# A visit's scores cut in two around the weighted sums, nine chunks as four rounds of eight tiles and one of four

## The chip, the cores and the metric

The kernel runs on one core of a Trainium2 chip. The metric is the device time of one execution in microseconds, the median of the timed runs. Lower is better.

## What is computed

The reference is a masked attention followed by a two-layer feed-forward network with a softplus between the layers:

```python
scores = scale * np.matmul(q, k.transpose(0, 1, 3, 2))        # B 8, H 8, S 576, D 64
rel = pos[:, None] - pos[None, :]
mask_local = (rel >= 0) & (rel < stride)                      # stride 32, heads 0 to 3
mask_strided = (rel >= 0) & (pos[None, :] % stride == pos[:, None] % stride)   # heads 4 to 7
attn = softmax(np.where(masks, scores, -1e9))
x = (attn @ v).transpose(0, 2, 1, 3).reshape(4608, 512)
h = x @ w_in                                                  # 512 x 2048
g = np.maximum(h, 0.0) + np.log1p(np.exp(-np.abs(h)))
out = g @ w_out                                               # 2048 x 512
```

Each query sees few keys, so the kernel computes only blocks of 32 queries by 64 keys on the diagonal. The host has put the queries and keys of the strided heads in an order in which their mask is such a band too.

## The kernel before

**The network.** The 4608 tokens are nine chunks of 512. A chunk takes 16 steps, one for each 128 columns of `w_in`. A step on TensorE (PE) is `hidden` (line 623: 12 matmuls of 128x512 into a tile `ph`) and, two steps later, `output` (line 663: 12 matmuls of 128x512 into the four tiles `py`). Between them ScalarE (ACT) makes abs, exp and ln of `ph` into `u` (lines 635 to 640), and VectorE (DVE) makes `u` = max(`ph`, 0) + `u` (line 644, the last reader of `ph`), then the rounded part `gh` (line 253) and the rest `gl` (line 656), which `output` reads. `ph` has two buffers (`ps_h`).

**The attention.** Heads are handled in pairs. There are 32 pairs, number n. The first eight are done in a first stage whose order is written out by hand. From n = 8 on a pair is a *visit* that the planner puts between a `hidden` and an `output`: one visit every three steps for n = 8 to 11, every four steps after that. A visit `S{n}` of n > 8 does two things on PE: the scores of pair n (`score_steps`, line 343) and the weighted sums of pair n - 1 (`weighted`, line 519, 12 matmuls for each half of the sequence).

**The scores of a pair.** They are nine chunks. A chunk is four products of 64x32 by 64x64 in fp32: two heads (rows 0 to 63 or 64 to 127 of PE's array) times two places (columns). In the trace each product is two matmuls. `SPLIT = [(0, 6), (6, 9)]`: chunks 0 to 5 go into the tile `ps`, chunks 6 to 8 into the upper half of `po`, whose lower half takes the sums' first half. The second sums' half goes to `pv`, a buffer of `ps_h`. The two parts are issued side by side: chunks 0 and 6, 1 and 7, 2 and 8, then 3, 4 and 5 alone. `place_of` swaps the heads' columns for the second part, so that chunks 0 and 6 together use eight different tiles of the array (two row halves times four column quarters), while a chunk alone uses four.

**Behind the scores** DVE adds the mask to each part (`add_mask`, line 409) into `prob`, takes the row maxima (line 414), subtracts them (line 418); ACT takes exp; DVE sums (line 428), inverts and multiplies (line 440), and turns `prob` into `pt` by transposes of 32 rows (line 451), one for each run of chunks with the same column order: 16 a pair, in two groups of eight with a `u`, `gh`, `gl` behind each. The next visit's sums read `pt`. Behind the sums ACT copies each half to `x_h` (line 557) and DVE writes the rest, `x_l` (line 555). The `ph` of the `hidden` behind the visit's `output` waits for DVE.

**The order.** `Plan` takes tasks with an urgency, an engine, a cost and what they come after, places each at the earliest gap on its engine, and issues all by the start that results. The tasks here are `S{n}` (PE), `Y{n}{j}` (the masks, DVE), `x s E z g R M` (the softmax), `P{n}.{j}` (transposes), `H` and `L` (`x_h` and `x_l`).

Of the kernel before, what the change touches and what calls it, by code (L numbers as in the profile page):

```python
# [10 lines left out]
F32 = mybir.dt.float32  # L11
F32R = mybir.dt.float32r
BF16 = mybir.dt.bfloat16
# [6 lines left out]
P = 128  # L20
# [3 lines left out]

TILE = 96
SPLIT = [(0, 6), (6, 9)]


def block_at(chunk, place):

    return (chunk, 2 * place) if chunk < 6 else (3 * place + chunk - 6, 1)
# [48 lines left out]
class Plan:  # L80
# [8 lines left out]
    def add(self, name, urgency, engine, cost, fn, after=(), late=0.0):  # L89
        self.tasks[name] = (urgency, len(self.tasks), engine, cost, fn, after, late)  # L90
# [29 lines left out]
def attention_softplus_ffn(  # L120
# [9 lines left out]
    nc = tc.nc  # L130
    B, NPAIR, _, _, S = qk.shape
# [7 lines left out]
    NCHK = NTILE * 3 // 2  # L139
# [20 lines left out]

    nc.scalar.preload_act_table_set("natural_log_exp_and_others")
    mask_b = const.tile([P, 12 * 64], BF16, name="mask_b")

# [9 lines left out]
    xs = {}  # L175
# [43 lines left out]
    def is_local(n):  # L219
        return order[n][1] < NPAIR // 2  # L220

    def q_of(n):
        return qT_early[n] if n < NPAIR else qT

    def k_of(n):
        return kT_early[n] if n < NPAIR else kT[n % 2]
# [66 lines left out]

    def mask_of(n, part):

        if is_local(n):
            return mask_b[:, : 6 * 64] if part == 0 else mask_b[:, 64 : 4 * 64]
        if part == 0:
            return mask_b[:, 6 * 64 : 9 * 64].unsqueeze(1).broadcast_to([P, 2, 3 * 64])
        return mask_b[:, 9 * 64 :]  # L300

    def place_of(n, part, h):

        return 1 - h if n >= NPAIR and part == 1 else h

    def score_steps(n, part):

        b = order[n][0]
        masked = b < 2
        if b == 0:  # L310
            ps = py[2 * (n % 2) + part]
        elif b == 1 or part == 0:
            taken.append(n)
            ps = ps_s.tile([P, 512], F32, tag="ps", name=f"ps_{n}_{part}")
        else:
            shared[n] = ps_o.tile([P, 512], F32, tag="po", name=f"po_{n}")
            ps = shared[n][:, S // 2 :]
        pss[n, part] = ps
        lo, hi = SPLIT[part]
        rows = [slice(64 * place, 64 * place + 64) for place in range(2)]  # L320

        def add(first):
            for place in range(2):
                nc.tensor.matmul(  # L324
                    ps[rows[place], : 64 * (hi - lo)],
                    lhsT=ident_b[:, rows[place]],
                    rhs=mask_of(n, part),
                    start=first,
                    stop=not first,
                )  # L330


        if masked and n > 0:
            add(True)
        for x in range(lo, hi):
            yield
            for place in range(2):
                a, i = block_at(x, place)
                c = TILE * a + 32 * i
                for h in range(2):  # L340
                    to = 64 * place + 32 * place_of(n, part, h)
                    head = slice(64 * h, 64 * h + 64)
                    nc.tensor.matmul(  # L343
                        ps[to : to + 32, 64 * (x - lo) : 64 * (x - lo) + 64],
                        lhsT=q_of(n)[head, c : c + 32],
                        rhs=k_of(n)[head, c : c + 64],
                        start=not masked or n == 0 and x == lo,
                        stop=not masked or n > 0 and x == hi - 1,
                    )
        if masked and n == 0:  # L350
            add(False)

    def scores(n, parts=range(2)):

        for _ in zip_longest(*[score_steps(n, part) for part in parts]):
            pass

    def parts(n, part=None):
        if n not in sts:
            sts[n] = st_pool.tile([P, 4, NCHK], F32, tag="stat", name=f"st_{n}")  # L360
        lo, hi = (0, NCHK) if part is None else SPLIT[part]
        sv = None
        if (n, part) in pss:
            sv = pss[n, part][:, : 64 * (hi - lo)].rearrange("p (a c) -> p a c", c=64)
        return prob_of(n)[:, lo:hi], sv, [sts[n][:, i, lo:hi] for i in range(4)]
# [36 lines left out]
    def add_mask(n, j):  # L402
        pv, sv, _ = parts(n, j)
        m = mask_of(n, j)
        if len(m.shape) == 3:
            pv, sv = (x.rearrange("p (two a) c -> p two (a c)", two=2) for x in (pv, sv))
        else:
            m = m.rearrange("p (a c) -> p a c", c=64)
        nc.vector.tensor_tensor(pv, sv, m, op=ALU.add)  # L409
        pss.pop((n, j))  # L410
# [31 lines left out]
    def prob_transposes(n, quarters=range(4)):  # L442
        p = prob_of(n)
        for quarter in quarters:
            for place, h in (divmod(quarter, 2),):
                for part, (lo, hi) in enumerate(SPLIT):
                    row = 64 * place + 32 * place_of(n, part, h)
                    src = p[row : row + 32]
                    a, i = block_at(lo, place)
                    for c in range(2):  # L450
                        nc.vector.transpose(  # L451
                            pt[
                                32 * (i + c) : 32 * (i + c) + 32,
                                h,
                                a : a + hi - lo,
                                32 * i : 32 * i + 32,
                            ],
                            src[:, lo:hi, 32 * c : 32 * c + 32],
                        )
# [42 lines left out]
    def weighted(n, half, joint=False):  # L502


        if joint:
            if half == 0:
                po = shared[n + 1]
            else:
                po = ps_h.tile([P, 512], F32, tag="ph", name=f"pv_{n}")
        elif half == 1 and (n == NPAIR - 1 or n >= 2 * NPAIR):  # L510
            taken.append(n)
            po = ps_s.tile([P, 512], F32, tag="ps", name=f"pv_{n}_{half}")
        else:
            po = ps_o.tile([P, 512], F32, tag="po", name=f"pv_{n}_{half}")
        pos[n, half] = po
        for x in range(NTILE // 2):
            a = NTILE // 2 * half + x
            for h in range(2):
                nc.tensor.matmul(  # L519
                    po[64 * h : 64 * h + 64, TILE * x : TILE * x + TILE],  # L520
                    lhsT=vs[n][:, a, h, :],
                    rhs=pt_of(n, a)[:, h, a % 2],
                    start=True,
                    stop=True,
                )
# [284 lines left out]
    for i in range(begin, len(steps) + LAG):  # L810
# [23 lines left out]
        for t in range(nt):  # L834
            name = f"O{k}" if t == nt - 1 else f"O{k}.{t}"
            after = [f"l{k}", before] + ([f"y{k-1}.{t}"] if f == 0 else [])
            add(name, x + 0.01 * t, "PE", 0.7, lambda c=c, f=f, t=t: output(c, f, (t,)), after)
            before = name
            if k == len(steps) - 1 and t == nt - 1:

                for h, (e, engine) in enumerate((("DVE", nc.vector), ("ACT", nc.scalar))):
                    cols = slice(DM // 2 * h, DM // 2 * (h + 1))
                    fn = lambda c=c, t=t, engine=engine, cols=cols: result(c, t, engine, cols)
                    add(f"y{k}.{t}{h}", x + 0.7 * t + 0.7, e, 0.35, fn, [name])
            elif f == NFC - 1:
                e, cost, engine = (("ACT", 0.5, nc.scalar), ("DVE", 0.6, nc.vector))[t % 2]
                fn = lambda c=c, t=t, engine=engine: result(c, t, engine)
                add(f"y{k}.{t}", x + 0.7 * t + 0.7, e, cost, fn, [name])
    def sums_of(n):
        for half in range(2):  # L850
            weighted(n, half, n != last)

    i_of = {n: i for i, n in pair_at.items()}
    for i, n in pair_at.items():
        x = when[i]
        if n > 2 * NPAIR:
            z = x - (when[i] - when[i - 2] if i - 2 in when else 0.0)
            add(f"Q{n}", z, "ACT", 2.5, lambda n=n: lay_out_q(n), [f"q{n}", f"S{n-1}"])
        after = [f"Q{n}", f"k{n}", f"Y{n-1}0", f"Y{n-1}1", f"L{n-2}1"]
        cost = 1.3  # L860
        if joint(i):
            cost = 2.5
            after += [f"P{n-1}", f"v{n-1}", f"u{i-1}"]

        def work(i=i, n=n):
            scores(n)
            if joint(i):
                sums_of(n - 1)

        add(f"S{n}", x, "PE", cost, work, after)  # L870
        y = x + 1.5
        for j in range(2):
            after = [f"S{n}", f"P{n-2}"]
            add(f"Y{n}{j}", y + j, "DVE", 0.47, lambda n=n, j=j: add_mask(n, j), after)
        after = [f"Y{n}0", f"Y{n}1"]
        for j, (letter, e, cost, fn) in enumerate(
            (
                ("x", "DVE", 0.75, row_maxima),
# [113 lines left out]
```

## Time and profile before

| | us |
|---|---|
| timed runs | 891.73, 892.96, 894.03 |
| median | 892.96 |
| span of the profiled execution, first to last instruction | 890.0 |
| PE busy in it | 879.5 |
| DVE, ACT, GpSimd busy | 575.0, 408.3, 56.1 |
| mean granted PE clock | 0.998 of full speed |

No whole time of the profiled execution is given beside its span: the median lies 2.96 us over the span. Row starts and durations of a timeline are in hundredths of a us; "x4" at the end of a row means that four instructions of one kind are merged, the start is the first one's and the duration reaches from its start to the last one's end. Matmuls overlap, so starts and not durations give PE's pace. PEld is PE's weight load.

### The profile page before, as it was taken

How to read it: one execution, taken by the hardware profiler on the slowest of the kernel's cores; microseconds unless marked ns; L12 is line 12 of the kernel's file. 1: busy time of each engine (PE TensorE's matmuls, PEld its weight loads, DVE VectorE, ACT ScalarE, POOL GpSimd, SP SyncE). 2: the span in 40 equal slices, each digit the busy share in tenths (PEclk: the TensorE clock that was granted, in tenths of full speed). 3: DMA queues.
4: the chain of work that ended last, by engine and by line, in shares of the span. 5: the costliest groups of instructions: out<-in, count | busy, mean ns of one | idle time of the engine just before them, and what ended most of it. 6: DMA issues, size and time to landing. Idle time of an engine off the chain costs nothing.

```text
span 890.0 us, 16587 instructions
## 1 busy us (share of the span) xinstructions
PE 879.5 (99%) x6786; PEld 719.0 (81%) x6786; DVE 575.0 (65%) x1264; ACT 408.3 (46%) x767; POOL 56.1 (6%) x84
## 2 busy tenths in 40 slices
PE   7999999999999999999999999999999999999998
PEld 5777778888888888888888888888888888888886
DVE  5878876778767777776766676677777333333332
ACT  6998655354443344344444344334433333333332
POOL 3354340000000000000000000000000000000000
PEclk9999999999999999999999999999999999999999
DMA  9856212222211112111211121111200010001001
GB/s 334 290 201 242 76 34 75 59 60 60 83 37 31 44 53 84 45 31 45 92 45 45 44 92 31 29 43 53 84 18 18 1 48 1 0 1 48 1 1 47
DMA packets 50091, 58.41 MB, mean 66 GB/s; under 512 B 3168, under 2 KB 35296, under 8 KB 50016
## 3 DMA queue, kind: packets, MB, share of 16 engines
q1 hardware_dynamic: 49728, 57.03, 19.8%
q8 instruction: 53, 0.87, 0.4%
q10 hardware_dynamic: 288, 0.33, 0.1%
q14 instruction: 22, 0.18, 0.1%
HBM read 47.91 MB, written 9.44 MB: 64 GB/s over the span
## 4 chain that ended last, share of the span: by engine, by line
PE 96%; DMA 1%; ACT 1%; DVE 1%; issue 0%; SPq 0%; ACTq 0%
PE py L663 45%; PE ph L623 44%; PE ps L343 3%; PE pv L519 2%; PE po L519 2%; DMA raw_q<-in_qk_dram 1%; PE po L343 0%; ACT early_l L392 0%; PE pt L489 0%; PE ps L324 0%; DVE a_i L594 0%; ACT pt L253 0%; ACT early_h L253 0%; ACT a_o L583 0%; DVE x_l L555 0%
## 5 line engine op out<-in xcount | busy, mean ns | idle before, releaser
L663 PE MATMUL py<-w_o,gh 128*128 128x512 f32 x1152 | 358.4, 392 | 0.0
L623 PE MATMUL ph<-x_h,w_i 128*128 128x512 f32 x1152 | 355.6, 390 | 0.0
L635 ACT ACTIVATE u<-ph 128x512 f32<-128x512 f32 x144 | 86.3, 600 | 399.5 <-PE ph L623 399.2
L623 PEld LDWEIGHTS ph<-x_h,w_i 128*128 128x128 f32 x1152 | 215.7, 188 | 45.4 <-issue 0.2
L663 PEld LDWEIGHTS py<-w_o,gh 128*128 128x128 f32 x1152 | 213.9, 188 | 46.7
L663 PE MATMUL py<-w_o,gl 128*128 128x512 f32 x576 | 224.4, 390 | 0.0
L623 PE MATMUL ph<-x_l,w_i 128*128 128x512 f32 x576 | 224.1, 389 | 0.0
L644 DVE SCALAR_TENSOR_TENSOR u<-ph,u 128x512 f32<-128x512 f32 x144 | 99.3, 689 | 173.2 <-ACT u L640 171.4
L451 DVE STREAM_TRANSPOSE pt<-prob 32x192 f32<-32x192 f32 x448 | 140.2, 317 | 6.8
L663 PEld LDWEIGHTS py<-w_o,gl 128*128 128x128 f32 x576 | 108.2, 188 | 22.7
L623 PEld LDWEIGHTS ph<-x_l,w_i 128*128 128x128 f32 x576 | 108.1, 188 | 22.5
L656 DVE TENSOR_TENSOR gl<-u,gh 128x512 fp32r<-128x512 f32 x136 | 94.3, 694 | 12.3 <-ACT gh L253 1.4
L638 ACT ACTIVATE u<-u 128x512 f32<-128x512 f32 x144 | 91.4, 635 | 4.4
L640 ACT ACTIVATE u<-u 128x512 f32<-128x512 f32 x144 | 91.0, 632 | 4.4
L253 DVE CAST gh<-u 128x512 fp32r<-128x512 f32 x128 | 54.4, 426 | 10.2
L409 DVE TENSOR_TENSOR prob<-ps,mask_b 128x384 f32<-128x384 f32 x24 | 13.4, 558 | 51.4 <-PE ps L343 51.4
L253 ACT COPY qT<-prob 128x576 f32<-128x576 f32 x28 | 35.9, 1283 | 0.7 <-DMA prob<-in_qk_dram 0.7
L424 ACT ACTIVATE prob<-prob 128x576 f32<-128x576 f32 x24 | 16.5, 687 | 39.2 <-DVE prob L418 39.2
L343 PEld LDWEIGHTS ps<-kT,qT 64*32 64x32 f32 x1440 | 24.8, 106 | 9.7 <-issue 9.3
L343 PE MATMUL ps<-kT,qT 64*32 64x64 f32 x1440 | 30.0, 221 | 0.0
L555 DVE TENSOR_TENSOR x_l<-pv,x_h 128x288 fp32r<-128x288 f32 (+2 forms) x47 | 18.8, 412 | 9.3 <-ACT x_h L557 9.1
L557 ACT CAST x_h<-pv 128x288 fp32r<-128x288 f32 (+2 forms) x47 | 16.8, 375 | 11.9 <-PE pv L519 11.7
(96 smaller groups left out, 486.6 us busy)
## 6 DMA issues: line engine op xcount, KB each, us to landing
v_in<-in_v_dram SPq DMA_DIRECT2D x28, 320.0 KB, 3.5
out_dram<-o SPq DMA_DIRECT2D x35, 256.0 KB, 2.1
ri<-in_moe_w_in_dram SPq DMA_DIRECT2D x16, 512.0 KB, 7.1
ro<-in_moe_w_out_dram SPq DMA_DIRECT2D x16, 512.0 KB, 7.3
kT<-in_qk_dram SPq DMA_DIRECT2D x28, 288.0 KB, 3.3
prob<-in_qk_dram SPq DMA_DIRECT2D x28, 288.0 KB, 2.8
v_in<-in_v_dram SPq DMA_DIRECT2D x28, 48.0 KB, 3.3
room<-in_v_dram SPq DMA_DIRECT2D x4, 320.0 KB, 6.6
```

The costliest lines, as they stand in the source:

```text
L253: (engine.copy if engine is nc.scalar else engine.tensor_copy)(dst, src)
L343: nc.tensor.matmul(ps[to : to + 32, 64 * (x - lo) : 64 * (x - lo) + 64], lhsT=q_of(n)[head, c : c + 32], rhs=k_of(n)[head, c : c + 64], st ...
L451: nc.vector.transpose(pt[32 * (i + c) : 32 * (i + c) + 32, h, a : a + hi - lo, 32 * i : 32 * i + 32,], src[:, lo:hi, 32 * c : 32 * c + 32],)
L519: nc.tensor.matmul(po[64 * h : 64 * h + 64, TILE * x : TILE * x + TILE], lhsT=vs[n][:, a, h, :], rhs=pt_of(n, a)[:, h, a % 2], start=True, ...
L555: nc.vector.tensor_tensor(place("l"), cut(lo, hi), high, op=ALU.subtract)
L623: nc.tensor.matmul(ph, lhsT=w32["i", f][:, half, cc * P : (cc + 1) * P], rhs=x_of(x, cc)[:, t0 : t0 + n], start=(i == 0), stop=(i == 3 * N ...
L635: nc.scalar.activation(us[c, f], phs[c, f], AF.Abs)
L638: nc.scalar.activation(u, u, AF.Exp, scale=-1.0)
L640: nc.scalar.activation(u, u, AF.Ln, bias=1.0)
L644: nc.vector.scalar_tensor_tensor(u, in0=phs.pop((c, f)), scalar=0.0, in1=u, op0=ALU.max, op1=ALU.add)
L656: engine.tensor_tensor(g, us.pop((c, f)), ghs[c, f].bitcast(F32), op=ALU.subtract)
L663: nc.tensor.matmul(py[t], lhsT=g[:, sl], rhs=w32["o", f][:, half], start=(f == 0 and n == 0), stop=(f == NFC - 1 and n == 2),)
```

## The change

From n = 8 on the scores go in five rounds, `ROUNDS = [(0, 5), (1, 6), (2, 7), (3, 8), (4,)]`, and a visit issues two rounds, then the weighted sums, then the other three. For the rounds to use eight tiles, chunk 5 gets the swapped columns too (from n = 9 on), and so becomes a part of its own: `CUTS = [(0, 5), (6, 9), (5, 6)]`, chunks 0 to 4 in `ps`, 6 to 8 in `po` as before, and chunk 5 in the upper half of `pv`, which is therefore taken at the start of the visit. The mask is added in three pieces. For strided heads a five-chunk mask is laid out once by two GpSimd copies (`mask_5`). The transposes have three runs of chunks instead of two: 24 a pair instead of 16.

```diff
+TURNED = 5
+CUTS = [(0, 5), (6, 9), (5, 6)]
+ROUNDS = [(0, 5), (1, 6), (2, 7), (3, 8), (4,)]
+EARLY_ROUNDS = 2
...
-        return 1 - h if n >= NPAIR and part == 1 else h
+        first = NCHK if n < NPAIR else SPLIT[1][0] if n <= 2 * NPAIR else TURNED
+        return 1 - h if x >= first else h
...
+    def score_rounds(n, rounds):
+
+        m = S // 2
+        if rounds[0] == ROUNDS[0]:
+            taken.append(n)
+            pss[n, 0] = ps_s.tile([P, 512], F32, tag="ps", name=f"ps_{n}_0")
+            shared[n, 0] = ps_o.tile([P, 512], F32, tag="po", name=f"po_{n}")
+            pss[n, 1] = shared[n, 0][:, m:]
+            if n > 2 * NPAIR:
+                shared[n, 1] = ps_h.tile([P, 512], F32, tag="ph", name=f"pv_{n}")
+                pss[n, 2] = shared[n, 1][:, m:]
+        for x in (x for xs in rounds for x in xs):
...
-                for part, (lo, hi) in enumerate(SPLIT):
-                    row = 64 * place + 32 * place_of(n, part, h)
+                cuts = sorted({0, SPLIT[1][0], NCHK} | ({TURNED} if n >= 2 * NPAIR else set()))
+                for lo, hi in zip(cuts, cuts[1:]):
+                    row = 64 * place + 32 * place_of(n, lo, h)
...
-            if half == 0:
-                po = shared[n + 1]
-            else:
-                po = ps_h.tile([P, 512], F32, tag="ph", name=f"pv_{n}")
+            po = shared[n + 1, half]
...
         def work(i=i, n=n):
-            scores(n)
+            score_rounds(n, ROUNDS[:EARLY_ROUNDS])
             if joint(i):
                 sums_of(n - 1)
+            score_rounds(n, ROUNDS[EARLY_ROUNDS:])
...
-        for j in range(2):
+        for j in range(len(cuts_of(n))):
             after = [f"S{n}", f"P{n-2}"]
-            add(f"Y{n}{j}", y + j, "DVE", 0.47, lambda n=n, j=j: add_mask(n, j), after)
+            add(f"Y{n}{j}", y + 0.6 * j, "DVE", 0.4, lambda n=n, j=j: add_mask(n, j), after)
```

What the scheduler makes of it on PE, in the visit of n = 19 (scores of 19, sums of 18). Before, from the last matmul of the `hidden` ahead of it to the first ones of the `output` behind it; a row with "32x64 x4" is one chunk:

```order
L623 MATMUL ph_10_4221<-x_l_670,w_i_1016 128x512
L343 MATMUL ps_0_4238<-kT_101,qT 32x64 x4
L343 MATMUL po_4239<-kT_101,qT 32x64 x4
L343 MATMUL ps_0_4238<-kT_101,qT 32x64 x4
L343 MATMUL po_4239<-kT_101,qT 32x64 x4
L343 MATMUL ps_0_4238<-kT_101,qT 32x64 x4
L343 MATMUL po_4239<-kT_101,qT 32x64 x4
L343 MATMUL ps_0_4238<-kT_101,qT 32x64 x12
L519 MATMUL po_4239<-pt,v_in 64x96 x6
L519 MATMUL pv_4282<-pt,v_in 64x96 x6
L663 MATMUL py_104<-w_o_1433,gh_8_4200 128x512 x2
```

The same place of the changed kernel:

```order
L389 MATMUL ps_0_4339<-kT_102,qT 32x64 x4
L389 MATMUL pv_4341<-kT_102,qT 32x64 x4
L389 MATMUL ps_0_4339<-kT_102,qT 32x64 x4
L389 MATMUL po_4340<-kT_102,qT 32x64 x4
L556 MATMUL po_4340<-pt,v_in 64x96 x6
L556 MATMUL pv_4341<-pt,v_in 64x96 x6
L389 MATMUL ps_0_4339<-kT_102,qT 32x64 x4
L389 MATMUL po_4340<-kT_102,qT 32x64 x4
L389 MATMUL ps_0_4339<-kT_102,qT 32x64 x4
L389 MATMUL po_4340<-kT_102,qT 32x64 x4
L389 MATMUL ps_0_4339<-kT_102,qT 32x64 x4
L700 MATMUL py_105<-w_o_1434,gh_8_4301 128x512 x2
```

The number of products is the same (36 for the scores, 12 for the sums). The sums stand behind the fourth chunk instead of the ninth, the visit ends with scores, and the last chunk of `ps` is the last thing that it does.

On DVE, behind the same visit: the masks, `x_l` of both halves with the row maxima between, and `u` of the `hidden` ahead of the visit. Before:

```order
L409 TENSOR_TENSOR prob<-ps_0_4238,mask_b 128x384
L409 TENSOR_TENSOR prob<-po_4239,mask_b 128x192
L555 TENSOR_TENSOR x_l_581<-po_4239,x_h_579 128x288
L414 TENSOR_REDUCE st_4306<-prob 128x9
L555 TENSOR_TENSOR x_l_581<-pv_4282,x_h_579 128x288
L644 SCALAR_TENSOR_TENSOR u_10_4289<-ph_10_4221,u_10_4289 128x512
```

The changed kernel:

```order
L448 TENSOR_TENSOR prob<-ps_0_4339,mask_90 128x320
L448 TENSOR_TENSOR prob<-po_4340,mask_b 128x192
L448 TENSOR_TENSOR prob<-pv_4341,mask_b 128x64
L592 TENSOR_TENSOR x_l_582<-po_4340,x_h_580 128x288
L453 TENSOR_REDUCE st_4407<-prob 128x9
L592 TENSOR_TENSOR x_l_582<-pv_4341,x_h_580 128x288
L681 SCALAR_TENSOR_TENSOR u_10_4390<-ph_10_4322,u_10_4390 128x512
```

The order of the tasks is the same, and one more mask addition of 64 columns stands between.

More of the change, by code (lines that the diff above doesn't have):

```diff
@@ L162, in attention_softplus_ffn @@
     mask_b = const.tile([P, 12 * 64], BF16, name="mask_b")
+    mask_5 = const.tile([P, 5 * 64], BF16, name="mask_5")
     early = {
@@ L294, in mask_of, with place_of, cuts_of @@
     def mask_of(n, part):
+        lo, hi = cuts_of(n)[part]
         if is_local(n):
-            return mask_b[:, : 6 * 64] if part == 0 else mask_b[:, 64 : 4 * 64]
-        if part == 0:
-            return mask_b[:, 6 * 64 : 9 * 64].unsqueeze(1).broadcast_to([P, 2, 3 * 64])
-        return mask_b[:, 9 * 64 :]
-    def place_of(n, part, h):
-        return 1 - h if n >= NPAIR and part == 1 else h
+            first = lo if lo < 6 else lo - 5
+            return mask_b[:, first * 64 : (first + hi - lo) * 64]
+        if hi - lo == 5:
+            return mask_5
+        if hi - lo > 3:
+            return mask_b[:, 6 * 64 : 9 * 64].unsqueeze(1).broadcast_to([P, 2, 3 * 64])
+        first = 9 if lo == 6 else 6 + lo % 3
+        return mask_b[:, first * 64 : (first + hi - lo) * 64]
+    def place_of(n, x, h):
+        first = NCHK if n < NPAIR else SPLIT[1][0] if n <= 2 * NPAIR else TURNED
+        return 1 - h if x >= first else h
+    def cuts_of(n):
+        return CUTS if n > 2 * NPAIR else SPLIT
     def score_steps(n, part):
         b = order[n][0]
-        masked = b < 2
         if b == 0:
             ps = py[2 * (n % 2) + part]
-        elif b == 1 or part == 0:
+        else:
             taken.append(n)
             ps = ps_s.tile([P, 512], F32, tag="ps", name=f"ps_{n}_{part}")
-        else:
-            shared[n] = ps_o.tile([P, 512], F32, tag="po", name=f"po_{n}")
-            ps = shared[n][:, S // 2 :]
         pss[n, part] = ps
@@ L330, in add @@
                 )
-        if masked and n > 0:
+        if n > 0:
             add(True)
@@ L340, in score_steps @@
                 for h in range(2):
-                    to = 64 * place + 32 * place_of(n, part, h)
+                    to = 64 * place + 32 * place_of(n, x, h)
                     head = slice(64 * h, 64 * h + 64)
@@ L346, in score_steps @@
                         rhs=k_of(n)[head, c : c + 64],
-                        start=not masked or n == 0 and x == lo,
-                        stop=not masked or n > 0 and x == hi - 1,
+                        start=n == 0 and x == lo,
+                        stop=n > 0 and x == hi - 1,
                     )
-        if masked and n == 0:
+        if n == 0:
             add(False)
@@ L356, in scores @@
             pass
+    def score_rounds(n, rounds):
[9 more added lines that the diff above has]
+        for x in (x for xs in rounds for x in xs):
+            part, lo = next((j, lo) for j, (lo, hi) in enumerate(cuts_of(n)) if lo <= x < hi)
+            cols = slice(64 * (x - lo), 64 * (x - lo) + 64)
+            for place in range(2):
+                a, i = block_at(x, place)
+                c = TILE * a + 32 * i
+                for h in range(2):
+                    to = 64 * place + 32 * place_of(n, x, h)
+                    head = slice(64 * h, 64 * h + 64)
+                    nc.tensor.matmul(
+                        pss[n, part][to : to + 32, cols],
+                        lhsT=q_of(n)[head, c : c + 32],
+                        rhs=k_of(n)[head, c : c + 64],
+                        start=True,
+                        stop=True,
+                    )
     def parts(n, part=None):
@@ L360, in parts @@
             sts[n] = st_pool.tile([P, 4, NCHK], F32, tag="stat", name=f"st_{n}")
-        lo, hi = (0, NCHK) if part is None else SPLIT[part]
+        lo, hi = (0, NCHK) if part is None else cuts_of(n)[part]
         sv = None
@@ L505, in weighted @@
         if joint:
-            if half == 0:
-                po = shared[n + 1]
-            else:
-                po = ps_h.tile([P, 512], F32, tag="ph", name=f"pv_{n}")
+            po = shared[n + 1, half]
         elif half == 1 and (n == NPAIR - 1 or n >= 2 * NPAIR):
@@ L848, in attention_softplus_ffn, with more_masks @@
                 add(f"y{k}.{t}", x + 0.7 * t + 0.7, e, cost, fn, [name])
+    def more_masks():
+        nc.gpsimd.tensor_copy(mask_5[:, : 3 * 64], mask_b[:, 6 * 64 : 9 * 64])
+        nc.gpsimd.tensor_copy(mask_5[:, 3 * 64 :], mask_b[:, 6 * 64 : 8 * 64])
+    add("masks", 0.0, "POOL", 0.5, more_masks)
     def sums_of(n):
@@ L858, in attention_softplus_ffn @@
             add(f"Q{n}", z, "ACT", 2.5, lambda n=n: lay_out_q(n), [f"q{n}", f"S{n-1}"])
-        after = [f"Q{n}", f"k{n}", f"Y{n-1}0", f"Y{n-1}1", f"L{n-2}1"]
+        after = [f"Q{n}", f"k{n}", f"Y{n-1}0", f"Y{n-1}1", f"Y{n-1}2", f"L{n-2}1"]
         cost = 1.3
@@ L865, in work @@
         def work(i=i, n=n):
-            scores(n)
+            score_rounds(n, ROUNDS[:EARLY_ROUNDS])
             if joint(i):
                 sums_of(n - 1)
+            score_rounds(n, ROUNDS[EARLY_ROUNDS:])
         add(f"S{n}", x, "PE", cost, work, after)
         y = x + 1.5
-        for j in range(2):
+        for j in range(len(cuts_of(n))):
             after = [f"S{n}", f"P{n-2}"]
-            add(f"Y{n}{j}", y + j, "DVE", 0.47, lambda n=n, j=j: add_mask(n, j), after)
-        after = [f"Y{n}0", f"Y{n}1"]
+            add(f"Y{n}{j}", y + 0.6 * j, "DVE", 0.4, lambda n=n, j=j: add_mask(n, j), after)
+        after = [f"Y{n}{j}" for j in range(len(cuts_of(n)))]
         for j, (letter, e, cost, fn) in enumerate(
```

## Prediction

> **What bounds the kernel now.** I read the page first: the span, the busy times, the chain that ended last, and the group of the weighted sums' first halves, which counts the visits.
>
> ```profile
> PE 879.5 (99%) x6786; PEld 719.0 (81%) x6786; DVE 575.0 (65%) x1264; ACT 408.3 (46%) x767; POOL 56.1 (6%) x84
> ...
> PE 96%; DMA 1%; ACT 1%; DVE 1%; issue 0%; SPq 0%; ACTq 0%
> ...
> L519 PE MATMUL po<-pt,v_in 128*64 128x96 f32 x276 | 16.5, 254 | 0.0
> ```
>
> PE is busy 99% of the span and carries 96% of the chain. So the change is worth what it takes out of PE's row, less any wait that it newly puts there. A visit's first half of sums is 12 matmuls, and 276 / 12 = 23: that many visits hold scores and sums. Everything below is one visit times 23.
>
> Second, PE's timeline through one visit (n = 19), from its first score to the `output` behind it and the next `hidden`.
>
> ```profile
> 383.83 0.26 PE L343 MATMUL ps<-kT,qT 64*32 64x64 f32 x4
> ...
> 383.91 0.24 PE L343 MATMUL ps<-kT,qT 64*32 64x64 f32 x4
> ...
> 383.96 0.24 PE L343 MATMUL ps<-kT,qT 64*32 64x64 f32 x4
> ...
> 384.02 0.24 PE L343 MATMUL ps<-kT,qT 64*32 64x64 f32 x4
> 384.05 0.24 PE L343 MATMUL po<-kT,qT 64*32 64x64 f32 x4
> 384.09 0.34 PE L343 MATMUL ps<-kT,qT 64*32 64x64 f32 x5
> ...
> 384.24 0.22 PE L343 MATMUL ps<-kT,qT 64*32 64x64 f32 x1
> ...
> 384.25 0.22 PE L343 MATMUL ps<-kT,qT 64*32 64x64 f32 x1
> ...
> 384.27 0.24 PE L343 MATMUL ps<-kT,qT 64*32 64x64 f32 x2
> ...
> 384.35 0.49 PE L343 MATMUL ps<-kT,qT 64*32 64x64 f32 x20
> 384.77 0.72 PE L519 MATMUL po<-pt,v_in 128*64 128x96 f32 x12
> 385.32 0.67 PE L519 MATMUL pv<-pt,v_in 128*64 128x96 f32 x12
> 385.91 0.73 PE L663 MATMUL py<-w_o,gh 128*128 128x512 f32 x2
> ...
> 388.77 0.62 PE L623 MATMUL ph<-x_h,w_i 128*128 128x512 f32 x2
> ```
>
> Every product is two matmuls, so a round has two passes. The first round's passes start at 383.83 and 383.91, the second's at 383.96 and 384.02, the third at 384.09. A round of eight tiles at full pace is thus 0.11 to 0.13 us. The third is slower: its `ps` chunk has eight matmuls, five from 384.09 on, then 384.24 and 384.25, and the eighth is the first of the two at 384.27, 0.18 after the first. At two passes of 0.06 it would have been done by 384.17. The last 20 `ps` matmuls are five passes of four: they start at 384.35, and the last one ends at 384.84, so at 0.22 each it starts at 384.62. That is 0.056 from pass to pass, the pace of four tiles alone. So what the third round loses is not PE's arithmetic. Two rounds are 16 products, 32 matmuls with 32 weight loads, 64 instructions. My reading is a window of 64 instructions that are issued and not finished: the 65th follows only when the first have ended, and these end 0.24 to 0.26 after their start (the first row: 0.26 over four). 383.83 + 0.26 = 384.09, which is when the third round begins.
>
> The Trainium skill, "TensorE: Matmul & The Clock Gate" (Part 1, the paragraph on engine queue depths), gives TensorE a queue of 64 instructions that is a partial reorder window. It does not say whether a place comes free at issue or at the end; what each would make of the time follows below.
>
> **The change on PE, part by part.** The last of the 32 early matmuls ends at 384.05 + 0.24 = 384.29 and so starts at 384.07. Before, from the last score's start (384.62) to the first sum (384.77) are 0.15. A pass takes 0.06 of that, and 0.09 is the switch from 64x32 tiles to 128x64.
>
> - Two rounds, then the switch: the sums would start at 384.07 + 0.15 = 384.22.
> - The sums themselves and the switch behind them are not changed: from 384.77 to 385.91, 1.14. The other scores would start at 385.36.
> - Rounds three and four behind the sums: 24 sums at 1.14 / 24 = 0.05 each give the queue a whole us to fill, so I take these two rounds at the pace of the first two. They are again 64 instructions.
> - The last round, chunk 4 alone, is then where the third round's `ps` chunk stood: behind 64 instructions. If it waits in the same way, its last matmul starts 384.27 - 383.83 = 0.44 after the first of the three rounds, at 385.80. At full pace it would be 0.19 (384.02 - 383.83) to the fourth pass, two more passes of 0.056 and 0.02 within the last: 0.32.
> - A switch again, 0.15: `output` starts at 385.95, or at 385.83 at full pace. Before it is 385.91.
>
> So PE's visit costs +0.04 by the row that stands behind the same 64 instructions, and -0.08 without that wait. Each of these is added up from hundredths that were mostly rounded up; I take +0.03. The gain of the rounds (five instead of six, 0.11) and of a queue that refills is spent on one more switch (0.09) and on the last round's wait. 23 x 0.03 = 0.7 us; the other end is 23 x -0.08 = -1.9 us.
>
> The first visit (n = 8) has scores without sums and no swapped chunk 5, so its first round is two chunks on the same four tiles; that is one more pass pair, once, 0.1 us.
>
> **What covers the rest.** On DVE and ACT three things get later: the masks, `x_l` and the transposes. The rows behind the same visit:
>
> ```profile
> 384.88 0.56 DVE L409 TENSOR_TENSOR prob<-ps,mask_b 128x384 f32<-128x384 f32 x1 [2.40 <-PE ps L343]
> 386.17 0.36 DVE L409 TENSOR_TENSOR prob<-po,mask_b 128x192 f32<-128x192 f32 x1 [0.74 <-ACT x_h L557]
> 386.45 0.45 DVE L555 TENSOR_TENSOR x_l<-po,x_h 128x288 fp32r<-128x288 f32 x1
> 386.81 0.74 DVE L414 TENSOR_REDUCE st<-prob 128x9 f32<-128x576 f32 x1
> 387.47 0.45 DVE L555 TENSOR_TENSOR x_l<-pv,x_h 128x288 fp32r<-128x288 f32 x1
> 387.84 0.68 DVE L644 SCALAR_TENSOR_TENSOR u<-ph,u 128x512 f32<-128x512 f32 x1
> ...
> 392.19 2.64 DVE L451 STREAM_TRANSPOSE pt<-prob 32x192 f32<-32x192 f32 x8
> 394.86 0.69 DVE L644 SCALAR_TENSOR_TENSOR u<-ph,u 128x512 f32<-128x512 f32 x1
> ...
> 396.90 2.54 DVE L451 STREAM_TRANSPOSE pt<-prob 32x192 f32<-32x192 f32 x8
> ```
>
> ```profile
> 385.76 0.38 ACT L557 CAST x_h<-po 128x288 fp32r<-128x288 f32 x1
> 386.04 0.40 ACT L557 CAST x_h<-pv 128x288 fp32r<-128x288 f32 x1
> ```
>
> ```profile
> L451 DVE STREAM_TRANSPOSE pt<-prob 32x192 f32<-32x192 f32 x224 | 81.6, 364 | 3.5
> L451 DVE STREAM_TRANSPOSE pt<-prob 32x96 f32<-32x96 f32 x224 | 60.5, 270 | 3.3
> ...
> L409 DVE TENSOR_TENSOR prob<-ps,mask_b 128x384 f32<-128x384 f32 x24 | 13.4, 558 | 51.4 <-PE ps L343 51.4
> ...
> L409 DVE TENSOR_TENSOR prob<-po,mask_b 128x192 f32<-128x192 f32 x24 | 8.6, 358 | 17.4 <-ACT x_h L557 17.4
> ```
>
> The `hidden` behind the visit's `output` starts 388.77 - 385.91 = 2.86 after that `output` and needs a `ph` buffer. It is the one that `pv` had, which `x_l`<-`pv` frees last, before at 387.47 + 0.45, 2.01 after the `output`'s start. Count from the `output`'s new start. The last `ps` score starts 0.15 ahead of it and ends 0.07 behind; before, the mask followed that end by 0.04 (384.84 to 384.88), so 0.11. Mask additions cost (558 - 358) / 192 = 1.04 ns a column: 0.49 for 320 columns, 0.22 for 64. Back to back an operation starts 0.08 before the last one ends (386.17 + 0.36 to 386.45). So the masks start at 0.11, 0.52 and 0.80, `x_l`<-`po` at 0.94, the maxima 0.36 later, `x_l`<-`pv` another 0.66 later at 1.96, ending at 2.41. Against 2.86 that leaves 0.45, and its weights, loaded 0.22 ahead of the matmul, still 0.2. Where an `x_l` is in two pieces (below) 0.2 more goes, and the cover is just used up. ACT's `x_h`<-`po` now also waits for chunk 8's score in the same bank: 385.36 + 0.24 + 0.22, about 385.86 instead of 385.76; the masks that wait for the two `x_h` start later than these end.
>
> Transposes: one of 160 columns and one of 32 in the place of one of 192. At (364 - 270) / 96 = 0.98 ns a column these are 333 and 207 instead of 364, so 0.18 more, eight times a pair: 1.4 us of DVE a visit. Who waits for them:
>
> ```profile
> 396.93 0.62 PE L663 MATMUL py<-w_o,gh 128*128 128x512 f32 x2
> ...
> 408.84 0.72 PE L519 MATMUL po<-pt,v_in 128*64 128x96 f32 x12
> ```
>
> ```profile
> 175.16 0.69 DVE L644 SCALAR_TENSOR_TENSOR u<-ph,u 128x512 f32<-128x512 f32 x1
> ...
> 182.25 0.68 DVE L644 SCALAR_TENSOR_TENSOR u<-ph,u 128x512 f32<-128x512 f32 x1
> ```
>
> ```profile
> 178.05 0.26 PE L343 MATMUL ps<-kT,qT 64*32 64x64 f32 x4
> ```
>
> The next sums start at 408.84, 9.4 after the last transpose (396.90 + 2.54); 0.4 of late masks and 1.4 come off that. The `u` of 387.84 feeds the `output` of 396.93. Both are covered. Tightest is `pv`, now taken with the first round: it needs the `u` of the `hidden` before last. Where visits are three steps apart that `u` ends at 175.85 and would end 1.8 later, at 177.7, against 178.05. Covered by 0.35; without that cover it would cost some tenths at each of the three-step visits. GpSimd's two mask copies run once, on an engine that is 6% busy.
>
> **The sum**: 890.0 + 0.7 for the profiled span, and on the median, which lies 2.96 higher, 892.96 + 0.7 = 893.7. That is under 0.3% (2.7 us), about what a measurement of this kernel can tell from no change.
>
> **Rivals.**
>
> *The last round does not wait* (a place in the queue is free at issue, or the third round's delay is a single hiccup). Then a visit costs -0.08 and the time is 892.96 - 1.9 = 891.1. For it: nothing in the rows shows why the delay must come back behind the sums. Against it: 383.83 + 0.26 fits so well. By the Trainium skill's page on TensorE read in the plain way, places freed as instructions leave, this is the forecast. Chance 0.22.
>
> *The `hidden` behind the visit waits for `u`.* If it takes not `pv`'s buffer but that of the `hidden` ahead of the visit, the one that frees it is `u`, which ends 0.36 + 0.68 after `x_l`<-`pv` begins: 1.96 + 1.04 = 3.0 against 2.86. PE would stand 0.15 and more a visit, with the 0.03 some 4 us: 897, slower. It decides as soon as `u` ends later than 2.86. Against it a visit whose `u` ran later:
>
> ```profile
> 182.76 0.41 PEld L623 LDWEIGHTS ph<-x_h,w_i 128*128 128x128 f32 x2
> ```
>
> The weights were loaded at 182.76 and that `u` ended at 182.93. Chance 0.07.
>
> *Rounds three and four do not run at full pace behind the sums*, because the queue is not full again. A round of eight then costs 0.18 as the third did before, two of them 0.1 more than planned; 23 x 0.13 = 3 us, 896. Chance 0.08.
>
> **How the numbers follow.** My forecast has 0.55, the rivals 0.22, 0.07 and 0.08, and 0.08 is left for what I don't see, either way. The forecast and the first rival lie within 0.3% save for noise: no change 0.72. Slower takes the two other rivals and half of the rest, 0.16. Faster by over 0.3% needs -0.12 a visit, a little more than the first rival gives: 0.12. The range reaches from the first rival less half a us of noise, 890.5, to the third rival, 896.0.
>
> **What would show it.** In the changed kernel's timeline the sums start 0.39 after the first score, the scores behind them 1.14 later, and `output` about 2.1 after the first score (now 2.08). The last chunk's eight matmuls straggle over 0.18, as those from 384.09 to 384.27 do. The `hidden` behind the visit still starts 2.86 after its `output`, with no wait for DVE. I am wrong if that start moves, if the visit is shorter than 2.03, or if rounds three and four take more than 0.13 each.

## The result, and the profile after

The changed kernel is slower, not unchanged: 908.02 us median (906.87 to 908.33, 4 runs) against 893.5 (891.73 to 894.62, 4 runs). The ratio is 1.0163, 95% interval 1.0148 to 1.0179, some 14.5 us: small, but well outside the spread of the runs. The forecast was +0.7 us and the range ended at 896.0.

First the visit, since the forecast was a visit times 23. PE's timeline of the changed kernel (start, duration, engine, line), the visit of n = 19, from its first score to the next `hidden`:

```profile
389.92 0.26 PE L389 MATMUL ps<-kT,qT 64*32 64x64 f32 x4
...
390.06 0.24 PE L389 MATMUL ps<-kT,qT 64*32 64x64 f32 x4
...
390.31 0.72 PE L556 MATMUL po<-pt,v_in 128*64 128x96 f32 x12
...
391.45 0.26 PE L389 MATMUL ps<-kT,qT 64*32 64x64 f32 x4
...
391.58 0.24 PE L389 MATMUL ps<-kT,qT 64*32 64x64 f32 x4
...
391.72 0.39 PE L389 MATMUL ps<-kT,qT 64*32 64x64 f32 x8
392.04 0.73 PE L700 MATMUL py<-w_o,gh 128*128 128x512 f32 x2
...
394.70 0.40 PE L700 MATMUL py<-w_o,gl 128*128 128x512 f32 x1
394.94 0.62 PE L660 MATMUL ph<-x_h,w_i 128*128 128x512 f32 x2
```

The sums start 0.39 after the first score, the scores again 1.14 later, and `output` 2.12 after the first score: the forecast to a hundredth. One number is off: the `hidden` starts 394.94 - 392.04 = 2.90 behind the `output`, where 2.86 was to stand. DVE's rows behind the same visit say whether it waits for DVE:

```profile
392.14 0.49 DVE L448 TENSOR_TENSOR prob<-ps,mask 128x320 f32<-128x320 f32 x1 [3.69 <-PE ps L389]
392.55 0.35 DVE L448 TENSOR_TENSOR prob<-po,mask_b 128x192 f32<-128x192 f32 x1
392.82 0.21 DVE L448 TENSOR_TENSOR prob<-pv,mask_b 128x64 f32<-128x64 f32 x1
392.95 0.45 DVE L592 TENSOR_TENSOR x_l<-po,x_h 128x288 fp32r<-128x288 f32 x1
...
393.97 0.45 DVE L592 TENSOR_TENSOR x_l<-pv,x_h 128x288 fp32r<-128x288 f32 x1
```

`x_l`<-`pv`, which frees the buffer, ends at 394.42, half a us before the `hidden`, and the `hidden` follows the last `gl` matmul (394.70) by 0.24, about as far as one matmul follows another in this `output` (394.23 to 394.70 are two). So PE does not wait. The 0.04 are in the twelve matmuls of `output` themselves, which the change did not touch. The four groups of network matmuls on the profile's page show it (line, shape, count, busy us, mean ns), before:

```profile
L663 PE MATMUL py<-w_o,gh 128*128 128x512 f32 x1152 | 358.4, 392 | 0.0
L623 PE MATMUL ph<-x_h,w_i 128*128 128x512 f32 x1152 | 355.6, 390 | 0.0
...
L663 PE MATMUL py<-w_o,gl 128*128 128x512 f32 x576 | 224.4, 390 | 0.0
L623 PE MATMUL ph<-x_l,w_i 128*128 128x512 f32 x576 | 224.1, 389 | 0.0
```

and after:

```profile
PE 892.8 (99%) x6786; PEld 717.7 (79%) x6786; DVE 603.2 (67%) x1479; ACT 410.2 (45%) x767; POOL 56.3 (6%) x86
...
PE 96%; DMA 1%; ACT 1%; DVE 1%; issue 0%; SPq 0%; ACTq 0%
...
L700 PE MATMUL py<-w_o,gh 128*128 128x512 f32 x1152 | 365.3, 398 | 0.0
L660 PE MATMUL ph<-x_h,w_i 128*128 128x512 f32 x1152 | 357.9, 392 | 0.0
...
L700 PE MATMUL py<-w_o,gl 128*128 128x512 f32 x576 | 227.3, 395 | 0.0
L660 PE MATMUL ph<-x_l,w_i 128*128 128x512 f32 x576 | 226.0, 392 | 0.0
```

There are as many matmuls, and the groups' busy times add up to 1176.5 us in place of 1162.5: 14.0 more, with PE still busy 99% and on 96% of the chain. With 23 x 0.03 for the visits that is 14.7 of the span's 15.1. It isn't the granted clock (spans and clock, before and after):

```profile
core 0: 890.0 us, clock 0.998
```

```profile
core 0: 905.1 us, clock 1.000
```

Nor does it happen only near the visits. In the last 190 us there are no visits, and DVE and ACT have the same operations in both kernels. There a step is twelve `py` matmuls and twelve `ph` ones; PE's timeline, the first row of each twelve, before:

```profile
747.05 0.62 PE L663 MATMUL py<-w_o,gh 128*128 128x512 f32 x2
...
749.77 0.62 PE L623 MATMUL ph<-x_h,w_i 128*128 128x512 f32 x2
...
752.49 0.62 PE L663 MATMUL py<-w_o,gh 128*128 128x512 f32 x2
```

and after:

```profile
748.51 0.64 PE L700 MATMUL py<-w_o,gh 128*128 128x512 f32 x2
...
751.31 0.62 PE L660 MATMUL ph<-x_h,w_i 128*128 128x512 f32 x2
...
754.06 0.64 PE L700 MATMUL py<-w_o,gh 128*128 128x512 f32 x2
```

A step takes 5.55 in place of 5.44; the `py` half 2.80 for 2.72, the `ph` half 2.75 for 2.72. So 227 ns from matmul to matmul became 233 and 229, in code that is the same. What differs for these matmuls? The order of the work around them, and one thing that the diff hides in a line: the new tile `mask_5`, 5 x 64 bf16 numbers, 640 bytes of each partition. Tiles lie in SBUF, the on-chip memory, in the order in which the kernel makes its pools and tiles. The profile shows no addresses; those here are worked out from that order and the tiles' sizes. `gh` and `gl` are first. Between them and x lie the tiles of `const`, 21248 bytes in the kernel before, which is 83 x 256; x takes 8 x 6144. Everything behind `mask_b`, x and the weights among them, lies 640 bytes higher than before.

### The profile page after: what moved, and what is told of

Same layout as the page of the kernel before. It is cut to its first block, busy times and chain, and to the rows that moved or that the text cites. A ratio compares the mean times of both kernels' runs of the same rounds, so it can differ in the third digit from the quotient of the medians.

```text
span 905.1 us, 16795 instructions
## 1 busy us (share of the span) xinstructions
PE 892.8 (99%) x6786; PEld 717.7 (79%) x6786; DVE 603.2 (67%) x1479; ACT 410.2 (45%) x767; POOL 56.3 (6%) x86
## 4 chain that ended last, share of the span: by engine, by line
PE 96%; DMA 1%; ACT 1%; DVE 1%; issue 0%; SPq 0%; ACTq 0%
PE py L700 45%; PE ph L660 44%; PE pv L556 2%; PE ps L389 2%; PE po L556 2%; DMA raw_q<-in_qk_dram 1%; PE ps L354 1%; PE po L389 0%; ACT early_l L431 0%; PE pt L529 0%; PE ps L335 0%; DVE a_i L631 0%; ACT pt L258 0%; ACT early_h L258 0%; ACT a_o L620 0%
## 5 line engine op out<-in xcount | busy, mean ns | idle before, releaser
L700 PE MATMUL py<-w_o,gh 128*128 128x512 f32 x1152 | 365.3, 398 | 0.0
L700 PE MATMUL py<-w_o,gl 128*128 128x512 f32 x576 | 227.3, 395 | 0.0
L491 DVE STREAM_TRANSPOSE pt<-prob 32x96 f32<-32x96 f32 (+3 forms) x640 | 167.8, 270 | 8.7
L448 DVE TENSOR_TENSOR prob<-ps,mask_b 128x320 f32<-128x320 f32 (+1 forms) x12 | 6.0, 497 | 38.5 <-PE ps L389 38.5
L448 DVE TENSOR_TENSOR prob<-ps,mask 128x320 f32<-128x320 f32 x12 | 5.9, 492 | 37.3 <-PE ps L389 37.3
L389 PEld LDWEIGHTS ps<-kT,qT 64*32 64x32 f32 x968 | 18.4, 105 | 11.2 <-issue 8.5
L389 PE MATMUL ps<-kT,qT 64*32 64x64 f32 x968 | 26.0, 222 | 0.0
```

The source lines that it names most:

```text
L389: nc.tensor.matmul(pss[n, part][to : to + 32, cols], lhsT=q_of(n)[head, c : c + 32], rhs=k_of(n)[head, c : c + 64], start=True, stop=True,)
L491: nc.vector.transpose(pt[32 * (i + c) : 32 * (i + c) + 32, h, a : a + hi - lo, 32 * i : 32 * i + 32,], src[:, lo:hi, 32 * c : 32 * c + 32],)
L700: nc.tensor.matmul(py[t], lhsT=g[:, sl], rhs=w32["o", f][:, half], start=(f == 0 and n == 0), stop=(f == NFC - 1 and n == 2),)
```

## The experiments

Theory A: the addresses of the matmuls' operands set their pace. Theory B: the new order, with its longer DVE work, slows PE. The first two kernels have one without the other.

**e1_pad**: the kernel before, with the tile and without its use.

```diff
     mask_b = const.tile([P, 12 * 64], BF16, name="mask_b")
+    pad = const.tile([P, 5 * 64], BF16, name="pad")
```

> The kernel before with nothing changed but an unused 640-byte tile behind `mask_b`, so that every later SBUF tile lies where it lies in the kernel after: the old order of work, the new addresses. Theory A (the addresses of the matmuls' operands set their pace): the 128x512 matmuls of the tail follow each other at 226 to 241 ns (mean near 231) instead of 226 to 227, and the time is that of the kernel after less what the visits grew by, 907 +- 1 us. Theory B (the new order of work, with its 640 transposes more, slows the matmuls): nothing moves, 893.5 +- 1 us and 227 ns in the tail.

**e2_last**: the kernel after, with the mask behind all other tiles.

```diff
     io_pool = ctx.enter_context(tc.tile_pool(name="io", bufs=4))
+    last_pool = ctx.enter_context(tc.tile_pool(name="last", bufs=1))
...
-    mask_5 = const.tile([P, 5 * 64], BF16, name="mask_5")
+    mask_5 = last_pool.tile([P, 5 * 64], BF16, name="mask_5")
```

> The kernel after with `mask_5` as the last tile of SBUF, so that all others lie where they lie in the kernel before: the new order of work, the old addresses. Theory A: the pace returns to 227 ns, and what is left is the visits' own growth of 23 x 0.03 us: 894.2 +- 1 us. Theory B: 908 +- 1 us, and the tail's matmuls stay at a mean near 231 ns.

e1_pad took 905.84 us against 892.33 of the kernel before beside it (ratio 1.0145, 1.0122 to 1.0168); e2_last 893.02 (1.0001, 0.9987 to 1.0014). An unused tile brings nearly the whole loss; moving the used one takes it away. B is out. (The 640 that theory B speaks of are all the transposes of the kernel after; 192 of them are new.) The tail of e1_pad, then that of e2_last, the same rows as above:

```profile
746.91 0.64 PE L664 MATMUL py<-w_o,gh 128*128 128x512 f32 x2
...
749.70 0.62 PE L624 MATMUL ph<-x_h,w_i 128*128 128x512 f32 x2
...
752.46 0.64 PE L664 MATMUL py<-w_o,gh 128*128 128x512 f32 x2
```

```profile
748.85 0.62 PE L701 MATMUL py<-w_o,gh 128*128 128x512 f32 x2
...
751.57 0.62 PE L661 MATMUL ph<-x_h,w_i 128*128 128x512 f32 x2
...
754.28 0.62 PE L701 MATMUL py<-w_o,gh 128*128 128x512 f32 x2
```

A step takes 5.55 and 5.43. Which address counts? Two kernels move one operand each.

**e3_w_only** puts the 640 bytes between the pools of x and of the weights, **e4_x_only** puts them ahead of x, and 1408 more behind x:

```diff
+    pad_pool = ctx.enter_context(tc.tile_pool(name="pad", bufs=1))
     w_pool = ctx.enter_context(tc.tile_pool(name="w", bufs=1))
...
+    pad = pad_pool.tile([P, 320], BF16, name="pad")
```

```diff
+    pad_pool = ctx.enter_context(tc.tile_pool(name="pad", bufs=1))
     x_pool = ctx.enter_context(tc.tile_pool(name="x", bufs=1))
+    rest_pool = ctx.enter_context(tc.tile_pool(name="rest", bufs=1))
     w_pool = ctx.enter_context(tc.tile_pool(name="w", bufs=1))
...
+    pad = pad_pool.tile([P, 320], BF16, name="pad")
+    rest = rest_pool.tile([P, 704], BF16, name="rest")
```

> The kernel before with the 640 bytes between the input's tiles and the weights' tiles: only `w_in` and `w_out` (and the small tiles behind them) move, x, q, k, v and the masks stay. Theory A splits in two. A1 (what counts is where the weights lie, `w_out` as the moving and `w_in` as the stationary operand): the whole of the 14 us comes back, 907 us, with the gh and gl matmuls near 233. A2 (what counts is the address of the moving operand alone, `w_out` for gh and gl, x for the others): about half, 897 to 903, with the `py` matmuls slow and the `ph` ones at 227. Theory B: 893.5.

> The kernel before with 640 bytes ahead of the input's tiles and 1408 behind them: x moves by 640, the weights by 2048, so that these keep their place within 2048 bytes. A1: 893.5 us, pace 227 ns. A2: about half of the loss, 897 to 903, with the `ph` matmuls slow and the `py` ones at 227. If the weights' whole address counts and not its remainder by 2048, the `py` matmuls are slow here too. Theory B: 893.5.

They took 912.38 us (ratio to the kernel before beside it 1.022, 95% interval 1.0194 to 1.0245) and 903.79 (1.0128, 1.0102 to 1.0155). Neither A1 nor A2 gives both: A2 nearly fits e4_x_only, but not e3_w_only. Against 892.33, moving the weights alone costs 20.1 us and moving x alone 11.5, where moving both together cost 13.5 (e1_pad). The tail of e3_w_only, then of e4_x_only:

```profile
748.25 0.63 PE L665 MATMUL py<-w_o,gh 128*128 128x512 f32 x2
...
751.04 0.63 PE L625 MATMUL ph<-x_h,w_i 128*128 128x512 f32 x2
...
753.84 0.63 PE L665 MATMUL py<-w_o,gh 128*128 128x512 f32 x2
```

```profile
746.08 0.63 PE L667 MATMUL py<-w_o,gh 128*128 128x512 f32 x2
...
748.81 0.62 PE L627 MATMUL ph<-x_h,w_i 128*128 128x512 f32 x2
...
751.60 0.63 PE L667 MATMUL py<-w_o,gh 128*128 128x512 f32 x2
```

With the weights moved both halves are slow, 2.79 and 2.80. With x moved `ph` is slow (2.79), `py` nearly clean (2.73). Each kind is slow where the distance changes between what it streams and what it loads as weights: `ph` streams x and loads `w_in`, `py` streams `w_out` and loads `gh` or `gl`. That is theory C. Its rival is D: the remainder of each tile's own address counts, by 512 or 1024. Four kernels are e3_w_only with another width of `pad`, **e5_w64**, **e6_w128**, **e7_w256**, **e8_w512** (the number is the bytes):

> As e3_w_only, with 64 bytes in place of 640 between the input and the weights. Theory C (from e1, e3 and e4: what counts is the distance between the addresses from which a matmul streams and from which the next weights are loaded; 640 is slow because it isn't a multiple of some unit): slow, 900 to 915 us, tail pace 229 to 238 ns, if the unit is 128 or more; 892.5 us and 227 ns if it is 64. Rival D (what counts is each tile's own remainder, by 512 or 1024, and any shift off it is slow, however small): 912 us, and all of the 128, 256 and 512 shifts the same.

> As e5 with 128 bytes. 640 is 512 + 128, so theory C with a unit of 256 or 512 gives just what 640 gave: 912 us, 229 to 238 ns for both kinds of matmuls; a unit of 128 can't be, since 640 is a multiple of it. D: 912 us too. If only the whole distance counts, something else.

> As e5 with 256 bytes. Theory C with a unit of 256: 892.5 us and 227 ns, since in the kernel before the `gl`/`gh` weights already lie 768 bytes off the `w_out` that streams (a multiple of 256, not of 512) and are fast. With a unit of 512 for the `ph` matmuls alone: these slow, the `py` ones fast. D: 912 us.

> As e5 with 512 bytes. Theory C with a unit of 256 or 512: 892.5 us, 227 ns. D with a remainder by 1024: 912 us; by 512: 892.5.

They took 910.86 us (1.0208, 1.0179 to 1.0238), 913.13 (1.0234, 1.0204 to 1.0264), 892.79 (1.0003, 0.9992 to 1.0015) and 893.1 (1.0013, 1.0001 to 1.0024). So the unit is 256 bytes: 64 and 128 are slow, 256 and 512 are not. D as put is out, but a rival D', each tile's own remainder by 256, is not. The second of the next two kernels tests it; the first asks whether the place of the mask itself matters.

**e9_768**: the kernel after, the mask at its place, made 768 bytes wide. **e10_all**: the kernel before, with 640 unused bytes ahead of every tile.

```diff
-    mask_5 = const.tile([P, 5 * 64], BF16, name="mask_5")
+    mask_5 = const.tile([P, 6 * 64], BF16, name="mask_5")
...
-            return mask_5
+            return mask_5[:, : 5 * 64]
...
-        nc.gpsimd.tensor_copy(mask_5[:, 3 * 64 :], mask_b[:, 6 * 64 : 8 * 64])
+        nc.gpsimd.tensor_copy(mask_5[:, 3 * 64 : 5 * 64], mask_b[:, 6 * 64 : 8 * 64])
```

```diff
+    pad_pool = ctx.enter_context(tc.tile_pool(name="pad", bufs=1))
     g_pool = ctx.enter_context(tc.tile_pool(name="g", bufs=3))
...
+    pad = pad_pool.tile([P, 320], BF16, name="pad")
```

> The kernel after with `mask_5` at its place but 768 bytes wide, of which 640 are used: x and the weights move by 768, a multiple of 256, against `gh` and `gl`. Theory C (unit of 256): as e2_last, 892.5 to 893.7 us, tail pace 227 ns, with the mask still in the middle of the other tiles. If it was the place of the mask itself and not the distance, 908.

> The kernel before with the unused 640 bytes ahead of all tiles, `gh` and `gl` included: every tile's own remainder by 256 is 128 now, and every distance is what it was before. Theory C (the distance between streamed and loaded operand): 892.3 us, 227 ns. Rival D' (each operand's own remainder by 256, which e7 and e8 don't exclude): 912 us or more, 229 to 241 ns.

They took 893.03 us (1.0004, 0.9992 to 1.0015) and 892.75 (1.0002, 0.999 to 1.0014). With every tile 128 off a multiple of 256 but the distances as before, nothing is lost; the tail of e10_all:

```profile
748.39 0.62 PE L665 MATMUL py<-w_o,gh 128*128 128x512 f32 x2
...
751.11 0.62 PE L625 MATMUL ph<-x_h,w_i 128*128 128x512 f32 x2
...
753.83 0.62 PE L665 MATMUL py<-w_o,gh 128*128 128x512 f32 x2
```

D' falls, C stands. Two last widths, **e13_w32** and **e14_w192**, ask whether the size of the remainder or its sign matters, and whether any distance is faster:

> As e3_w_only with 32 bytes. Multiples of 256 stand at 227 ns, 64 at a mean of 232.2, 128 at 232.6. If the loss comes as soon as the distance is no multiple of 256: 908 to 913 us, a mean of 231 to 233 ns. If it grows with the remainder: between, 900 to 906. If there is a distance that is better than a multiple of 256, under 227 ns and under 892 us.

> As e3_w_only with 192 bytes, as far below a multiple of 256 as 64 is above one. If only the distance's size counts: as with 64, 911 us, `ph` 233 and `py` 231 ns. If it also counts which of the two operands lies ahead: other means, the sum still slow.

They took 915.83 us (1.0257, 1.0227 to 1.0287) and 910.32 (1.0195, 1.0166 to 1.0225). 32 bytes are the worst of all, so the loss doesn't grow with the remainder. 192 and 64 cost about the same, with the two kinds exchanged. Here are these runs side by side. The distance is that between the weights and x, and between the weights and `gh` or `gl`; the times are of different sessions, in which the kernel before took 892.3 to 893.5. The pace is the mean from one start to the next in the trace, where both are network matmuls less than 300 ns apart (1691 of each kind):

| kernel | remainder of the distance by 256: w - x, w - g | `ph` ns | `py` ns | us |
|---|---|---|---|---|
| before | 0, 0 | 226.8 | 227.2 | 893.5 |
| after | 0, 128 | 229.3 | 233.0 | 908.02 |
| e1_pad | 0, 128 | 229.2 | 232.7 | 905.84 |
| e2_last | 0, 0 | 226.9 | 227.4 | 893.02 |
| e3_w_only | 128, 128 | 232.6 | 232.6 | 912.38 |
| e4_x_only | 128, 0 | 232.7 | 227.9 | 903.79 |
| e13_w32 | 32, 32 | 233.4 | 233.1 | 915.83 |
| e5_w64 | 64, 64 | 233.3 | 231.2 | 910.86 |
| e6_w128 | 128, 128 | 232.6 | 232.6 | 913.13 |
| e14_w192 | 192, 192 | 230.4 | 233.4 | 910.32 |
| e7_w256, e8_w512 | 0, 0 | 226.9 | 227.2 | 892.79, 893.1 |
| e9_768 | 0, 0 | 226.8 | 227.4 | 893.03 |
| e10_all | 0, 0 | 226.8 | 227.2 | 892.75 |

Where only one kind is off, the other loses a little too: the first matmuls behind a slow twelve are still late. In the tail of e1_pad (behind 700 us) the first seven of twelve `ph` matmuls follow each other at a mean of 231 ns, the next four at 226.6 to 226.7, about as in the kernel before. In e4_x_only the first three of twelve `py` matmuls take 231 to 232, the others 227.

**The visit itself.** With the pace restored, two kernels move the cut between scores and sums in e2_last: three rounds ahead of the sums (**e11_early3**) and one (**e12_early1**).

```diff
-EARLY_ROUNDS = 2
+EARLY_ROUNDS = 3
```

> e2_last with three rounds of scores ahead of the sums in place of two. The window of 64 of the prediction: 96 instructions ahead of the sums, so the third round waits there (its last matmul starts 0.44 after the first score, the sums at 0.59), and 48 behind them, which don't wait: last score 0.15 behind the resumption at 1.73, `output` at 2.03 in place of 2.11, 1.9 us less in all, 891.1. If the wait of the last chunk in e2_last is not the queue's but that of four tiles alone, it stays: 2.11 or more, 893.

> e2_last with one round of scores ahead of the sums. The window of 64: 32 instructions ahead of the sums, no wait, sums 0.25 after the first score; behind them 112, of which the third round waits and the last chunk follows at pace: last score 0.5 behind the resumption at 1.39, `output` at 2.05 in place of 2.11, 1.4 us less, 891.6. Without the window: no waits at all, `output` at 2.00, 890.4.

They took 893.98 us (1.0016, 1.0005 to 1.0028) and 894.32 (1.0017, 1.0005 to 1.0029): no gain, and a little slower than the kernel before. PE's timeline of a visit in e11_early3:

```profile
313.83 0.26 PE L390 MATMUL ps<-kT,qT 64*32 64x64 f32 x4
...
314.10 0.34 PE L390 MATMUL ps<-kT,qT 64*32 64x64 f32 x5
314.22 0.25 PE L390 MATMUL po<-kT,qT 64*32 64x64 f32 x2
...
314.29 0.27 PE L390 MATMUL po<-kT,qT 64*32 64x64 f32 x4
314.49 0.72 PE L557 MATMUL po<-pt,v_in 128*64 128x96 f32 x12
...
315.63 0.26 PE L390 MATMUL ps<-kT,qT 64*32 64x64 f32 x4
...
315.77 0.29 PE L390 MATMUL ps<-kT,qT 64*32 64x64 f32 x8
315.99 0.50 PE L701 MATMUL py<-w_o,gh 128*128 128x512 f32 x1
```

and in e12_early1, from the first score to the `output`:

```profile
312.46 0.26 PE L390 MATMUL ps<-kT,qT 64*32 64x64 f32 x4
...
313.87 0.26 PE L390 MATMUL ps<-kT,qT 64*32 64x64 f32 x4
...
314.14 0.34 PE L390 MATMUL ps<-kT,qT 64*32 64x64 f32 x5
...
314.60 0.50 PE L701 MATMUL py<-w_o,gh 128*128 128x512 f32 x1
```

The late starts come where the window of 64 puts them: behind 32 matmuls with their weight loads, 0.27 after the first of them, ahead of the sums in e11_early3 and behind them in e12_early1. The last chunk of e11_early3 has fewer than 64 instructions between the sums and itself, and no longer straggles: its eight take 0.29 from 315.77 on, in the kernel after 0.39 from 391.72 on. My sizes were too small. A waiting round of 16 straggles over 0.24 (314.10 to 314.29 + 0.27 - 0.22, the last start); the 0.18 that I took was that of eight matmuls. From the first to the last start of the scores behind the sums of e11_early3 are 0.21, not 0.15, and in e12_early1 0.58, not 0.5. The visits took 2.15 (313.83 to 315.99, rounded) and 2.13 (312.46 to 314.60, rounded) in place of 2.03 and 2.05.

## Why the prediction was wrong

**The visit, 23 x 0.03.** Right. From the first score to `output` the visits take 2.113 us in the trace against 2.085 before, and as much with the other addresses (2.112 in e2_last, 2.085 in e1_pad); with the old addresses the `hidden` starts 2.87 behind the `output` (314.84 to 317.71 in e2_last), so a visit cost some 0.04 in all, 0.9 us. The time of e2_last, 893.02 against 892.33, is too near to show or exclude it.

**The window of 64.** Right about where PE waits: e11 and e12 moved the wait as it says, though the visits came out longer where shorter ones were forecast. The last chunk's eight matmuls straggle over 0.17 (0.39 - 0.22; forecast 0.18), so the first rival (the last round doesn't wait, 891.1) is out. The Trainium skill, "TensorE: Matmul & The Clock Gate" (Part 1, engine queue depths), has the 64. The 33rd matmul starts 0.27 after the first, 0.03 after the trace's end of the first (0.24), which fits a place that comes free only when an instruction ends. A limit of 32 matmuls would look the same, since each has one weight load; no run here separates the two.

**The DVE cover.** Right: masks at 0.10, 0.51 and 0.78 behind the `output` (forecast 0.11, 0.52, 0.80), `x_l`<-`pv` at 1.93 (1.96), no wait. The second rival is out. The third is out too: rounds three and four start at 391.45 and 391.58 and the last at 391.72, 0.13 and 0.14 apart, as the first two do (389.92, 390.06), which do not wait. (The text had named more than 0.13 as a sign of being wrong; that was set too near.)

**What failed** is a term that the sum put at nothing, without a line of its own. "Everything below is one visit times 23" took the 3456 network matmuls to be untouched, because no line of theirs changed. Their four groups add up to 1162.5 us (one matmul overlaps the next, so this is more than PE's 879.5): 1.2% on them is more than all that the visits could give or cost. The nearest that the text came to the cause was the sentence "GpSimd's two mask copies run once, on an engine that is 6% busy": it priced the writing of the mask and not its place. The tile's 640 bytes moved the streamed `w_out` from a multiple of 256 bytes off the loaded `gh` and `gl` to 128 beside one. That cost 14.0 us, and made a change that is worth nothing measurable into one that loses 1.6%. The sign that the text named for being wrong, a `hidden` that no longer starts 2.86 behind its `output`, did appear, but its 0.04 were pace and no wait.

Some slips in the working change none of this. 23 x 0.08 is 1.8, not 1.9, and 385.36 + 0.24 + 0.22 is 385.82, not 385.86. Slower, as the two rivals and half of the rest, would be 0.19, not 0.16. The range ends at the third rival's 896.0, although the second is priced at 897.

What would have shown that something moves there is a list of the places in SBUF of the costliest groups' operands, before and after. Its price was in no view: no row of the profile of before could have given it, since all its distances are multiples of 256.

**Open.** Why the distance counts is not shown. The weight loads run beside the stream (188 ns of each 227), so that the two reads of SBUF might get in each other's way at some distances; that is a guess, and no run tests it. Nor is it shown whether the load for the same matmul or for the next one is what meets the stream. Nor were operands of another type tried. No layout tried was faster than a multiple of 256, and no version beat the kernel before.

## What to carry to other kernels

A new tile is a change to every tile allocated behind it. Allocate it last, or round it up to a multiple of 256 bytes (e9_768: a tile made 128 bytes wider, 15 us less), and when matmuls slow down that nobody touched, look at where their operands lie before looking at the schedule. A kernel with the tile and without its use, and one with the use and the tile elsewhere, separate the two in two runs.

## What the runs showed of the hardware

- In this kernel (operands declared fp32r, one core) back-to-back 128x512 matmuls, weights loaded for each, follow each other at 227 ns in the mean when the streamed and the loaded operand lie a multiple of 256 bytes apart in their partition, and at 230 to 233 ns in the mean at remainders of 32, 64, 128 and 192. Single ones scatter from 224 to 241 in both cases; at a multiple of 256 most are 226 or 227. The distance counts, and not the addresses' own remainders by 256: with all tiles shifted by 640 bytes nothing is lost (e10_all).
- Between 32 and 192 the loss doesn't grow with the remainder: 915.83, 910.86, 913.13 and 910.32 us at 32, 64, 128 and 192, against 892.3 to 892.6 of the kernel before beside them. Each has two timed runs.
- The slow pace outlasts its cause by some matmuls (`ph` at a mean of 229 in e1_pad, where its own distance is a multiple of 256 but the `py` ahead of it is slow).
